# Three token groups share the first six slices of w_in; x of the third group at first in the place of the last four slices

## The chip, the cores and the metric

The kernel runs on one core of a Trainium2 chip. The metric is the device time of one execution in microseconds (us). Five runs of the kernel before took 668.6 to 671.58 us, median 669.63.

## The reference

A retention layer is followed by a feed-forward layer with SiLU. All inputs are float32 or wider; q, k and v have 4 batches, 8 heads, 768 positions and 64 features.

```python
for t in range(S):
    state = gamma * state + einsum('bhd,bhe->bhde', k[:, :, t], v[:, :, t])
    y[:, :, t] = scale * einsum('bhd,bhde->bhe', q[:, :, t], state)
x = y.transpose(0, 2, 1, 3).reshape(3072, 512)
h = x @ w_in                       # 512 x 2048
out = (h / (1 + exp(-h))) @ w_out  # 2048 x 512
```

## The kernel before, in words

The 768 positions are cut into six chunks of 128. One **unit** (c, b) is chunk c of batch b; there are 24 units, and the four units of a chunk make one **group** of 512 tokens. A **visit** (`visit`, L380) works on three units at once, in a pipeline: it transposes k and q of unit m (`stage_t`, TensorE, evacuated as kt and qt by ScalarE at L288), computes y of unit m-2 (`stage_y`), finishes that unit (`finish_y`), computes the scores sc of unit m-1 (`stage_a`, L334) and loads k and q two units ahead. So the units of group c are finished in visits 4c+2 to 4c+5.

[...] `split_x` (L359) makes from y the parts xh (ScalarE, L362), xl (VectorE, L363) and xm (VectorE, L364). All parts of one group's x lie in a tile xt of 128 x 3 x 4 x 512 words; the pool `xpool` has two of them. `take_w` converts a slice of the weights: `convert_w` (L172 to L186, one ScalarE and six VectorE instructions) turns 64-bit words into float32, and for w_in `split_w` (L105 to L110, two ScalarE and two VectorE instructions) splits it into wi. Slices 0 to 15 are the 16 slices of w_in, 16 to 31 those of w_out, which are only converted and written to memory (wod). Each w_in slice has its own place, tag `w0` to `w15`, in `wpool`; in the last group the split w_out slices (wo) take these places over, each after its last product.

`product_in(c, f)`, below product (c,f), multiplies group c with slice f: twelve matmuls of 512 columns into the PSUM tiles ha and hb (two of each), the first of which needs xh of all four units, the second xl and the third xm. ScalarE and VectorE evacuate them (L415, L416) into g, ScalarE applies Silu (L417), and `put_g` writes g to memory (gd, L423). The tile of g is one of three with the tag `hs` in `hpool`. After the last group, a second stage reads the g back, splits them (gs, L456 to L459) and multiplies with wo; it is not touched.

There are places for only two x tiles, and group 2 is finished in visits 10 to 13, before groups 0 and 1 are through. So group 2 is `LATE`: `finish_y` copies its y (ys, L348, a tile of tag `hs`) and writes it to memory (yd, L349); `late_x` (L371) later reads it back (yr, L375, again a tile of tag `hs`) and splits it into an xt tile, which is free once group 0 is through.

The order on TensorE is written by hand: it is the order of the calls. On ScalarE, VectorE, GpSimd and SyncE (SP, which issues the loads and most writes) a planner places the instructions when the kernel is built, the earlier traced first where several are ready; it may move them ahead of the calls around them. `issue_after(evac[0])` keeps a ScalarE instruction behind the last copy of qt that was traced. Each engine then works through its order strictly.

The order before: visits 0 to 5 with slices 0 to 3 come first. Then (0,0..7) with slices 4 to 10 and visits 6 to 10; (1,0..7) with slices 11 to 15 and visits 11 to 13; (0,8..15) with slices 16 and 17; (1,8..15) with slice 18, and `late_x` of unit 0 to 3 after (1,9), (1,10), (1,11) and (1,12). Groups 2 to 5 run through all 16 slices one after the other, with four visits in each and six slices of w_out in each of groups 2, 3 and 4, as far as there are any.

Of the kernel before, what the change touches and what calls it, by code (L numbers as in the profile page):

```python
# [13 lines left out]
FP32R = mybir.dt.float32r  # L14
U32 = mybir.dt.uint32
AF = mybir.ActivationFunctionType
# [10 lines left out]
HALF = 1.0 - 2.0 ** -13  # L27
# [4 lines left out]
def kernel(  # L32
# [26 lines left out]
    nc = tc.nc  # L59
    B, H, S, D = q.shape  # L60
    DM, DF = moe_w_in.shape
    C = 128
    NC = S // C
    HP = H // 2
    KIN = DM // 128
    NF = DF // 128
    NT = B * C
# [4 lines left out]
    scale = 1.0 / math.sqrt(D)  # L72
# [8 lines left out]
    wpool = pool("wpool", 1)  # L81
    xpool = pool("xpool", 2)
# [14 lines left out]
    def bits(x):  # L97
        return float(np.array(x, np.uint32).view(np.float32))

    def split_w(f, w32, name, factor):  # L100

        w = wpool.tile([128, 3, 512], FP32R, tag=f"w{f}", name=f"{name}{f}")
        lo = conv.tile([128, 512], FP32, tag="wl", name=f"{name}l_{f}")
        with tc.issue_after(evac[0]):
            nc.scalar.activation(out=w[:, 0, :], in_=w32, func=AF.Copy, scale=HALF * factor)  # L105
        high = w[:, 0, :].bitcast(FP32)
        nc.vector.scalar_tensor_tensor(out=lo, in0=w32, scalar=factor, in1=high,
                                       op0=ALU.mult, op1=ALU.subtract)
        nc.scalar.activation(out=w[:, 1, :], in_=lo, func=AF.Copy, scale=1.0 / EPS)
        nc.vector.scalar_tensor_tensor(out=w[:, 2, :], in0=high, scalar=EPS, in1=lo,  # L110
                                       op0=ALU.mult, op1=ALU.subtract)
        return w
# [73 lines left out]
        nc.vector.tensor_tensor(out=w, in0=s.bitcast(FP32), in1=p.bitcast(FP32), op=ALU.add)  # L186
        return w

    evac, w_sb = [], {}
    taken = [0]  # L190

    def take_w(between=lambda: None):
        i = taken[0]
        taken[0] += 1
        if i >= 2 * NF:
            return
        w32 = convert_w(i)
        between()
        if i < NF:
            w_sb[i] = split_w(i, w32, "wi", scale)  # L200
        else:
            nc.sync.dma_start(out=wo_dram[i - NF], in_=w32)
# [137 lines left out]
    def finish_y(n):  # L340
        c, b = units[n]
        sp, yp = live.pop(n)
        qt.pop(n)
        if b == 0 and c != LATE:
            xt[c] = xpool.tile([128, 3, KIN, NT], FP32R, tag="xt", name=f"xt_{c}")
        if c == LATE:
            y = hpool.tile([128, KIN, C], FP32, tag="hs", name=f"ys_{b}")
            nc.scalar.copy(out=y.rearrange("p (i o) t -> p i o t", o=2), in_=yp)  # L348
            nc.sync.dma_start(out=y_dram[b], in_=y)  # L349
            rest = None  # L350
        else:
            rest = split_x(c, b, yp)
        if c == 0:
            nc.scalar.copy(out=state[b], in_=sp)
        elif c < NC - 1:
            nc.vector.tensor_tensor(out=state[b], in0=state[b], in1=sp, op=ALU.add)
        return rest

    def split_x(c, b, y):  # L359
        xh, xl, xm = (xt[c][:, i, :, ts(b, C)].rearrange("p (i o) t -> p i o t", o=2)  # L360
                      for i in range(3))
        nc.scalar.activation(out=xh, in_=y, func=AF.Copy, scale=HALF)  # L362
        nc.vector.tensor_tensor(out=xl, in0=y, in1=xh.bitcast(FP32), op=ALU.subtract)  # L363
        return lambda: nc.vector.scalar_tensor_tensor(  # L364
            out=xm, in0=xl.bitcast(FP32), scalar=-1.0 / EPS, in1=xh.bitcast(FP32),
            op0=ALU.mult, op1=ALU.add)


    LATE = 2

    def late_x(b):  # L371
        if b == 0:
            xt[LATE] = xpool.tile([128, 3, KIN, NT], FP32R, tag="xt", name=f"xt_{LATE}")
        y = hpool.tile([128, KIN, C], FP32, tag="hs", name=f"yr_{b}")
        nc.sync.dma_start(out=y, in_=y_dram[b])  # L375
        split_x(LATE, b, y.rearrange("p (i o) t -> p i o t", o=2))()
# [3 lines left out]
    def visit():  # L380
        m = visits[0]
        visits[0] += 1
        if m - 2 >= len(units):
            return
        if m < len(units):
            stage_t(m)
        rest = None
        if m >= 2:
            stage_y(m - 2)
            rest = finish_y(m - 2)  # L390
        if 1 <= m <= len(units):
            stage_a(m - 1)
            scale_q(m - 1)
            scale_k(m - 1)
        if rest is not None:
            rest()
        load("k", m + 2)
        load("q", m + 2)
        load("v", m)
# [4 lines left out]
    def product_in(c, f):  # L404
        ha = ps_h.tile([128, 512], FP32, tag="ha", name=f"ha_{c}_{f}")
        hb = ps_h.tile([128, 512], FP32, tag="hb", name=f"hb_{c}_{f}")
        for kk in range(KIN):
            w = [w_sb[f][:, i, ts(kk, 128)] for i in range(3)]
            x = [xt[c][:, i, kk, :] for i in range(3)]
            first_, last = kk == 0, kk == KIN - 1  # L410
            nc.tensor.matmul(ha, lhsT=w[0], rhs=x[0], start=first_, stop=False)  # L411
            nc.tensor.matmul(ha, lhsT=w[1], rhs=x[1], start=False, stop=last)  # L412
            nc.tensor.matmul(hb, lhsT=w[2], rhs=x[2], start=first_, stop=last)  # L413
        hs = hpool.tile([128, NT], FP32, tag="hs", name=f"g_{c}_{f}")
        nc.scalar.activation(out=hs, in_=ha, func=AF.Copy, scale=ONE_E)  # L415
        nc.vector.tensor_tensor(out=hs, in0=hs, in1=hb, op=ALU.subtract)  # L416
        nc.scalar.activation(out=hs, in_=hs, func=AF.Silu)  # L417
        pending.append((c, f, hs))

    def put_g(keep):  # L420
        while len(pending) > keep:
            c, f, g = pending.pop(0)
            nc.sync.dma_start(out=g_dram[c, f], in_=g)  # L423
# [5 lines left out]
    def get(n):  # L429
        if n >= len(order):  # L430
            return
        c, f = order[n]
        name = "kqk"[n % 3]
        g = ld.tile([128, NT], FP32, tag=f"{name}f", name=f"gr_{c}_{f}",
                    bufs=4 if name == "k" else 2)
        nc.sync.dma_start(out=g, in_=g_dram[c, f])
        got[n] = g

    def get_w(f):
        if f < NF:  # L440
            t = stage.tile([128, DM], FP32, tag="wf", name=f"wr_{f}")
            nc.sync.dma_start(out=t, in_=wo_dram[f])
            w_got[f] = t
# [3 lines left out]
    def split(n):  # L447
        if n >= len(order):
            return
        c, f = order[n]  # L450
        get(n + G_AHEAD)
        g = got.pop(n)
        if f % 4 == 0:
            blocks[n // 4] = xpool.tile([128, 3, 4, NT], FP32R, tag="xt", name=f"gs_{c}_{f}")
        t = blocks[n // 4][:, :, f % 4, :]
        nc.scalar.activation(out=t[:, 0, :], in_=g, func=AF.Copy, scale=HALF)  # L456
        high = t[:, 0, :].bitcast(FP32)
        nc.vector.tensor_tensor(out=t[:, 1, :], in0=g, in1=high, op=ALU.subtract)  # L458
        nc.vector.scalar_tensor_tensor(out=t[:, 2, :], in0=t[:, 1, :].bitcast(FP32),  # L459
                                       scalar=-1.0 / EPS, in1=high,  # L460
                                       op0=ALU.mult, op1=ALU.add)
        ready[n] = t
# [8 lines left out]
    for m in range(1, B + 2):  # L471
# [2 lines left out]
            take_w()  # L474
        if m == 2:
            first_chunk()
    half = NF // 2
    phases = ((0, 0, (0, 1, 2, 3, 5), (0, 1, 2, 3, 4, 5, 6)),
              (1, 0, (1, 3, 5), (0, 1, 2, 3, 5)),
              (0, half, (), (2, 6)),  # L480
              (1, half, (), (7,)))
    for c, f0, at, takes in phases:
        for i in range(half):
            product_in(c, f0 + i)
            if i in takes:
                take_w()
            put_g(1)
            if i in at:
                visit()
            if (c, f0) == (1, half) and 1 <= i <= B:  # L490
                late_x(i - 1)
    for c in range(2, NC):
        for f in range(NF):
            product_in(c, f)
            if c < NC - 1 and f % 3 == 0:
                take_w()
            put_g(1)
            if f % 4 == 1:
                visit()
            if c == NC - 1:  # L500
                if f == 0:
                    get_w(0)
                    get_w(1)
                wo[f] = split_w(f, w_got.pop(f), "wo", 1.0)
                get_w(f + 2)
                if f >= NF - 6:
                    if f == NF - 6:
                        for n in range(G_AHEAD):
                            get(n)
                    if f >= NF - S_AHEAD:  # L510
                        split(f - NF + S_AHEAD)
    put_g(0)

    for c in range(NC):
# [56 lines left out]
```

## Time and profile before

| | |
|---|---|
| median of five runs | 669.63 us |
| the profiled execution | 669.77 us, span of its core 667.9 us |
| TensorE (PE) busy | 634.4 us, 95% |
| VectorE (DVE) busy | 424.3 us, 64% |
| ScalarE (ACT) busy | 281.8 us, 42% |
| mean granted TensorE clock | 0.992 |
| first product (0,0) starts | 40.26 us |

The profile shows one execution. Times are us from the start of the span. An instruction's line names the line of the kernel, the tile that it writes and the one that it reads (without their numbers: xt is any x tile, wi any w_in slice), and behind it, in brackets, how long its engine sat idle before it and what ended that. "PE" is TensorE's matmuls; their printed lengths overlap, so the distance of two starts is what one costs. The page cuts the span into 40 slices of 16.7 us, each digit the busy tenths of an engine. A busy average over the span says little here, as the stages differ.

### The profile page before, as it was taken

To read this page: it belongs to the slowest core of one execution; us is meant where nothing else is said; L and a number is where in the kernel's file an instruction comes from. 1 tells how busy PE (TensorE), PEld (TensorE's weight loads), DVE (VectorE), ACT (ScalarE), POOL (GpSimd) and SP (SyncE) were. 2 spreads that over 40 slices of the span, in tenths; PEclk is the share of its full clock that TensorE was granted. 3 is DMA by queue.
4 is the path that set the end of the run, shared out by engine and by line. 5 is a ranking of instruction groups with operands and counts; after the bars stand their busy time and mean duration, and the time that the engine had idled before them with its cause. 6 is when DMAs were issued, how large, how long until landed. Compare 5 with 4: busy or idle time off the path is not lost.

```text
span 667.9 us, 11107 instructions
## 1 busy us (share of the span) xinstructions
PE 634.4 (95%) x4288; PEld 518.6 (78%) x4288; DVE 424.3 (64%) x696; ACT 281.8 (42%) x510; POOL 10.5 (2%) x44
## 2 busy tenths in 40 slices
PE   4769988999999999999999999999999999999996
PEld 3657767787788888888888888888888888888885
DVE  4898999995558686866347777363555454544631
ACT  5535566554545444444436883132131312221311
POOL 3000000000000000000000000000000000000000
PEclk9979989999999999999999999999999999999999
DMA  9976767865456676755324664252333342523401
GB/s 205 196 163 168 186 189 195 236 227 211 142 174 204 181 222 185 219 176 189 126 80 143 221 196 140 74 162 91 126 126 127 110 143 75 177 82 107 159 0 64
DMA packets 123061, 103.50 MB, mean 155 GB/s; under 512 B 80000, under 2 KB 88192, under 8 KB 123008
## 3 DMA queue, kind: packets, MB, share of 16 engines
q1 hardware_dynamic: 119552, 96.49, 49.2%
q10 hardware_dynamic: 3456, 6.29, 2.5%
q8 instruction: 34, 0.56, 0.3%
q14 instruction: 19, 0.16, 0.1%
HBM read 66.06 MB, written 36.70 MB: 154 GB/s over the span
## 4 chain that ended last, share of the span: by engine, by line
PE 69%; DVE 12%; DMA 8%; ACT 6%; issue 3%; SPq 1%; ACTq 0%; DVEq 0%
PE ha L411 8%; PE hb L413 8%; PE ha L412 8%; PE ob L533 7%; PE o L533 6%; PE o L532 6%; PE o L531 6%; PE oa L531 6%; PE oa L532 6%; DMA wf<-in_moe_w_in_dram 3%; PE y L303 2%; DVE g L416 2%; PE tp L285 2%; DMA gd<-g 1%; DVE am L338 1%
## 5 line engine op out<-in xcount | busy, mean ns | idle before, releaser
L413 PE MATMUL hb<-xt,wi 128*128 128x512 f32 x384 | 151.4, 394 | 4.2 <-DVE xt L364 3.5
L411 PE MATMUL ha<-xt,wi 128*128 128x512 f32 x384 | 153.0, 398 | 0.4 <-ACT g L415 0.4
L412 PE MATMUL ha<-xt,wi 128*128 128x512 f32 x384 | 150.7, 392 | 0.0
L458 DVE TENSOR_TENSOR gs<-gr,gs 128x512 fp32r<-128x512 f32 x96 | 62.1, 686 | 93.4 <-ACT gs L456 93.4
L456 ACT ACTIVATE gs<-gr 128x512 fp32r<-128x512 f32 x96 | 53.3, 620 | 139.2 <-issue 131.9
L416 DVE TENSOR_TENSOR g<-g,hb 128x512 f32<-128x512 f32 x96 | 65.7, 684 | 60.5 <-ACT g L415 59.9
L413 PEld LDWEIGHTS hb<-xt,wi 128*128 128x128 f32 x384 | 72.5, 189 | 22.5 <-DVE xt L364 3.8
L417 ACT ACTIVATE g<-g 128x512 f32<-128x512 f32 x96 | 60.6, 632 | 69.5 <-DVE g L416 69.4
L411 PEld LDWEIGHTS ha<-xt,wi 128*128 128x128 f32 x384 | 72.5, 189 | 19.1 <-issue 3.6
L412 PEld LDWEIGHTS ha<-xt,wi 128*128 128x128 f32 x384 | 72.5, 189 | 14.7 <-DVE xt L363 0.3
L415 ACT ACTIVATE g<-ha 128x512 f32<-128x512 f32 x96 | 56.8, 591 | 54.2 <-PE ha L412 36.2
L533 PE MATMUL ob<-wo,gs 128*128 128x512 f32 x192 | 75.3, 392 | 0.0
L533 PE MATMUL o<-wo,gs 128*128 128x512 f32 x192 | 74.8, 390 | 0.0
L531 PE MATMUL oa<-wo,gs 128*128 128x512 f32 x192 | 74.8, 390 | 0.0
L532 PE MATMUL oa<-wo,gs 128*128 128x512 f32 x192 | 74.8, 390 | 0.0
L531 PE MATMUL o<-wo,gs 128*128 128x512 f32 x192 | 74.8, 390 | 0.0
L532 PE MATMUL o<-wo,gs 128*128 128x512 f32 x192 | 74.8, 390 | 0.0
L459 DVE SCALAR_TENSOR_TENSOR gs<-gs 128x512 fp32r<-128x512 f32 x96 | 61.9, 685 | 0.0
L533 PEld LDWEIGHTS ob<-wo,gs 128*128 128x128 f32 x192 | 36.1, 188 | 9.0 <-DVE o L539 1.7
L531 PEld LDWEIGHTS oa<-wo,gs 128*128 128x128 f32 x192 | 36.1, 188 | 7.6 <-ACT o L538 0.2
L532 PEld LDWEIGHTS o<-wo,gs 128*128 128x128 f32 x192 | 36.1, 188 | 7.5
L533 PEld LDWEIGHTS o<-wo,gs 128*128 128x128 f32 x192 | 36.1, 188 | 7.5
(67 smaller groups left out, 684.8 us busy)
## 6 DMA issues: line engine op xcount, KB each, us to landing
gd<-g SPq DMA_DIRECT2D x96, 256.0 KB, 3.0
gr<-gd SPq DMA_DIRECT2D x96, 256.0 KB, 2.7
wf<-in_moe_w_out_dram SPq DMA_DIRECT2D x16, 512.0 KB, 3.6
kf<-in_k_dram SPq DMA_DIRECT2D x24, 256.0 KB, 4.3
qf<-in_q_dram SPq DMA_DIRECT2D x24, 256.0 KB, 4.1
vf<-in_v_dram SPq DMA_DIRECT2D x24, 256.0 KB, 4.4
out_dram<-o ACTq DMA_DIRECT2D x24, 256.0 KB, 2.1
wf<-in_moe_w_in_dram SPq DMA_DIRECT2D x16, 256.0 KB, 3.1
```

Source lines behind the costliest of these rows:

```text
L411: nc.tensor.matmul(ha, lhsT=w[0], rhs=x[0], start=first_, stop=False)
L412: nc.tensor.matmul(ha, lhsT=w[1], rhs=x[1], start=False, stop=last)
L413: nc.tensor.matmul(hb, lhsT=w[2], rhs=x[2], start=first_, stop=last)
L415: nc.scalar.activation(out=hs, in_=ha, func=AF.Copy, scale=ONE_E)
L416: nc.vector.tensor_tensor(out=hs, in0=hs, in1=hb, op=ALU.subtract)
L417: nc.scalar.activation(out=hs, in_=hs, func=AF.Silu)
L456: nc.scalar.activation(out=t[:, 0, :], in_=g, func=AF.Copy, scale=HALF)
L458: nc.vector.tensor_tensor(out=t[:, 1, :], in0=g, in1=high, op=ALU.subtract)
L459: nc.vector.scalar_tensor_tensor(out=t[:, 2, :], in0=t[:, 1, :].bitcast(FP32), scalar=-1.0 / EPS, in1=high, op0=ALU.mult, op1=ALU.add)
L531: nc.tensor.matmul(oa, lhsT=gh, rhs=wo[f][:, 0, :], start=first_, stop=False)
L532: nc.tensor.matmul(oa, lhsT=glo, rhs=wo[f][:, 1, :], start=False, stop=last)
L533: nc.tensor.matmul(ob, lhsT=gm, rhs=wo[f][:, 2, :], start=first_, stop=last)
```

## The change

The 16 slices of w_in get 12 places of their own and one shared place `wq` of four slices, for slices 12 to 15; it has the size of one x tile. Group 2's x is split at once, as that of the other groups, into this place, and group 2 runs its first six products from there. After these, slices 12 to 15 are split into the place. y of group 2 is still written to memory, and read back and split a second time into an x tile, for its other ten products. The copy ys in on-chip memory is what the first split reads.

The order is now: (0,0..5), (1,0..5), (2,0..5), (0,6..10), (1,6..10), (0,11..15), (1,11..15), (2,6..15), then groups 3 to 5 as before. Visits 6 to 9 stand in the first of these, 10 to 13 in the second, 14 to 17 in the last. The slices are taken later: 4, 5, 6 in (0,0..5), 7 and 8 in (1,0..5), 9 and 10 in (2,0..5), then two in each of the next three stretches; slices 17 to 20 of w_out go beside (2,6..15), and the last five beside group 4. `late_x` follows (1,12), (1,13), (1,14) and (1,15). For slices 12 to 15 the first ScalarE instruction of the split is held behind the last traced xh in place of the last copy of qt; in the last group, the four w_out slices in `wq` can be written only when (5,15) is through with all four.

```diff
+    quads = {}
+    def w_slot(f, name):
+        if f < NF - 4:
+            return wpool.tile([128, 3, 512], FP32R, tag=f"w{f}", name=f"{name}{f}")
+        if f == NF - 4:
+            quads[name] = wpool.tile([128, 4, 3, 512], FP32R, tag="wq", name=f"{name}4")
+        return quads[name][:, f - NF + 4]
...
-        w = wpool.tile([128, 3, 512], FP32R, tag=f"w{f}", name=f"{name}{f}")
+        w = w_slot(f, name)
-        with tc.issue_after(evac[0]):
+        with tc.issue_after(held[0] if f >= NF - 4 else evac[0]):
...
-        if b == 0 and c != LATE:
-            xt[c] = xpool.tile([128, 3, KIN, NT], FP32R, tag="xt", name=f"xt_{c}")
+        if b == 0:
+            p, tag = (wpool, "wq") if c == LATE else (xpool, "xt")
+            xt[c] = p.tile([128, 3, KIN, NT], FP32R, tag=tag, name=f"xt_{c}")
         if c == LATE:
             y = hpool.tile([128, KIN, C], FP32, tag="hs", name=f"ys_{b}")
-            nc.scalar.copy(out=y.rearrange("p (i o) t -> p i o t", o=2), in_=yp)
+            y4 = y.rearrange("p (i o) t -> p i o t", o=2)
+            nc.scalar.copy(out=y4, in_=yp)
             nc.sync.dma_start(out=y_dram[b], in_=y)
-            rest = None
-        else:
-            rest = split_x(c, b, yp)
+            yp = y4
+        rest = split_x(c, b, yp)
...
-        nc.scalar.activation(out=xh, in_=y, func=AF.Copy, scale=HALF)
+        held[:] = [nc.scalar.activation(out=xh, in_=y, func=AF.Copy, scale=HALF).ins]
...
-    phases = ((0, 0, (0, 1, 2, 3, 5), (0, 1, 2, 3, 4, 5, 6)),
-              (1, 0, (1, 3, 5), (0, 1, 2, 3, 5)),
-              (0, half, (), (2, 6)),
-              (1, half, (), (7,)))
+    for c, f, takes, at in ((0, range(6), (0, 2, 5), (0, 1, 3, 4)),
+                            (1, range(6), (2, 5), (0, 1, 3, 4)),
+                            (2, range(6), (1, 4), ()),
+                            (0, range(6, 11), (7, 9), ()),
+                            (1, range(6, 11), (7, 9), ()),
+                            (0, range(11, NF), (11, 13), ()),
+                            (1, range(11, NF), (), ()),
+                            (2, range(6, NF), (6, 9, 12, 15), (6, 8, 11, 13))):
...
-            if (c, f0) == (1, half) and 1 <= i <= B:
-                late_x(i - 1)
+        if c == 1 and NF - B <= f:
+            late_x(f - NF + B)
```

More of the change, by code (lines that the diff above doesn't have):

```diff
@@ L187, in convert_w @@
         return w
-    evac, w_sb = [], {}
+    evac, held, w_sb = [], [], {}
     taken = [0]
@@ L476 @@
             first_chunk()
-    half = NF // 2
-    phases = ((0, 0, (0, 1, 2, 3, 5), (0, 1, 2, 3, 4, 5, 6)),
-              (1, 0, (1, 3, 5), (0, 1, 2, 3, 5)),
-              (0, half, (), (2, 6)),
-              (1, half, (), (7,)))
[L482 to L489, printed above, removed]
-            if (c, f0) == (1, half) and 1 <= i <= B:
-                late_x(i - 1)
@@ L492 @@
-    for c in range(2, NC):
-        for f in range(NF):
[L494 to L511, printed above, removed]
+    steps = {}
@@ new lines @@
+    for c, f, takes, at in ((0, range(6), (0, 2, 5), (0, 1, 3, 4)),
[6 more added lines that the diff above has]
+                            (2, range(6, NF), (6, 9, 12, 15), (6, 8, 11, 13))):
+        for i in f:
+            steps[c, i] = i in takes, i in at
@@ new lines @@
+    for c in range(3, NC):
+        for f in range(NF):
+            steps[c, f] = c < NC - 1 and f % 3 == 0, f % 4 == 1
+    for (c, f), (takes, at) in steps.items():
+        product_in(c, f)
+        if takes:
+            take_w()
+        put_g(1)
+        if at:
+            visit()
+        if c == 1 and NF - B <= f:
+            late_x(f - NF + B)
+        if c == NC - 1:
+            if f == 0:
+                get_w(0)
+                get_w(1)
+            wo[f] = split_w(f, w_got.pop(f), "wo", 1.0)
+            get_w(f + 2)
+            if f >= NF - 6:
+                if f == NF - 6:
+                    for n in range(G_AHEAD):
+                        get(n)
+                if f >= NF - S_AHEAD:
+                    split(f - NF + S_AHEAD)
```

## The prediction

> **What bounds the kernel now.** I read the page first, then the busy time by stretch, then TensorE's order of time with its waits, then those of SP and VectorE. The page gives TensorE 95%, and its slices say where the rest is:
>
> ```profile
> PE 634.4 (95%) x4288; PEld 518.6 (78%) x4288; DVE 424.3 (64%) x696; ACT 281.8 (42%) x510; POOL 10.5 (2%) x44
> ...
> PE   4769988999999999999999999999999999999996
> ...
> DVE  4898999995558686866347777363555454544631
> ...
> PEclk9979989999999999999999999999999999999999
> ```
>
> The chain that ended last is 69% TensorE, 12% VectorE (DVE). The average hides the stage of the change: TensorE is short of 9 in the slices up to 133 us, and there DVE shows 8 and 9. The table by stretch (busy us and instruction count for PE, PEld, DVE, ACT, POOL, then the clock and DMA) says it in us:
>
> ```profile
> 40.00:60.00 20.00, 15.38 (x180) 11.94 (x172) 16.90 (x28) 9.95 (x18) 0.00 (x0) 0.91 0.68 156
> 60.00:80.00 20.00, 18.92 (x250) 15.67 (x251) 19.59 (x36) 11.01 (x20) 1.36 (x1) 1.00 0.77 194
> 80.00:100.00 20.00, 17.73 (x142) 14.53 (x141) 19.06 (x34) 11.62 (x21) 0.00 (x0) 0.91 0.68 192
> ...
> 120.00:140.00 20.00, 18.68 (x152) 15.08 (x151) 19.37 (x35) 12.58 (x23) 1.09 (x1) 1.00 0.73 220
> ...
> 160.00:180.00 20.00, 19.50 (x84) 15.04 (x83) 9.55 (x15) 10.44 (x18) 0.00 (x0) 1.00 0.42 141
> 180.00:300.00 120.00, 119.39 (x1082) 98.24 (x1081) 84.64 (x142) 55.71 (x98) 2.19 (x2) 1.00 0.65 194
> ```
>
> From 60 to 140 DVE is full (18.6 to 19.6 of 20); from 180 on TensorE idles 0.6 us in 120. So only 40 to 140 can be won. Its waits (last bracket: idle, releaser), four of them:
>
> ```profile
> 44.75 0.50 PE L413 MATMUL hb<-xt,wi 128*128 128x512 f32 x1 [3.53 <-DVE xt L364]
> ...
> 52.96 1.10 PE L334 MATMUL sc<-qt,kt 64*64 64x128 f32 x32 [1.06 <-ACT qt L288]
> ...
> 86.93 1.96 PE L334 MATMUL sc<-qt,kt 64*64 64x128 f32 x32 [2.27 <-ACT qt L288]
> ...
> 115.51 1.10 PE L334 MATMUL sc<-qt,kt 64*64 64x128 f32 x32 [1.79 <-ACT qt L288]
> ```
>
> The first lies before anything that the change moves. The sc matmuls of visits 6 to 13 wait 1.06, 0, 0.98, 0, 2.27, 0.26, 1.79 and 1.31 us, 7.7 in all: ScalarE's copy of qt stands in its queue behind a Silu or a w split that waits for the full DVE. After the 2.27 the matmuls run at half rate until 90.27 (starts 0.43 apart, not 0.23), about 1.5 us more.
>
> **The early part: DVE load.** From rows: product 12 x 0.227 = 2.73 us of TensorE and 0.68 of DVE; visit 4.15 (64.00 to 69.13 less its wait), 4.28 with the slower first matmul behind it. A w_in slice costs DVE eight ops (0.44+0.42+0.69+0.42+0.70+0.68+0.69+0.69) = 4.7 us; a visit am 1.22, qt, kf, xl, xm 0.69 each, state 0.41 = 4.4; for group 2 it was 3.0 without the x split. Before, (0,0..7) asks DVE for 8 x 0.68 + 7 x 4.7 + 4 x 4.4 + 3.0 = 59 us beside 8 x 2.73 + 5 x 4.28 = 43 of TensorE. After: w4 is done at 49.7 as now, so (0,0..5) has w5, w6 and four visits, 4.1 + 9.4 + 17.6 = 31 beside 33.5; (1,0..5), the four added splits in it (4 x 1.37 DVE, 4 x 0.59 ACT), 31 beside 33.5; (2,0..5) 13.5 beside 16.4; (0,6..10) 12.8 beside 13.7. DVE fits, at 92%.
>
> - **Visit waits.** Bounds: only the 1.06 of visit 6 stays (ScalarE loads a table there), -6.6, or all stay, 0. I take 3.0 left (1.06 and seven of 0.28, the size of the 0.26 row), since visits still come in pairs: **-4.7**.
> - **The slow stretch at 87** goes with its gap: **-1.5** (0 if another gap replaces it).
> - **New joints.** (1,0) and (2,0) follow one product after the visit that ends their x. TensorE needs xm 4.15 + 2.86 + 0.46 = 7.5 us after the visit starts; xm ended 6.0 after (visit 14, quiet DVE), 7.0 (visit 6) and 11.6 (visit 9, full DVE). For (2,0) add 0.6, as x is split from the copied y. Bounds 0 and 4.1 + 4.7; slices w6 and w8 are fenced behind the visit's qt copy, so near visit 6: **+0.5**.
> - **Slices in time.** w8 to w15 may run back to back after visit 13 (w_out slice 19, traced after (2,0) at 179, finished at 156, so slices move ahead). At 6.4 us each (w13, w14, w15 ended 6.3 and 6.5 apart) and 5 for the visit, w15 is there 56 us after visit 13 starts; (0,15) starts at 4.28 (the visit) + 2.73 for (1,5) + 16.4 for (2,0..5) + 27.3 for (0,6..10) and (1,6..10) + 10.9 for (0,11..14) = 61.7. **0**; at 7.4 each (as 89.72 to 97.13) 2.5.
> - **Shared place.** w12's first ScalarE op waits for the last matmul of (2,5), and behind it stand evacuations; two buffers of ha and hb cover it: **0**, at most one product, 2.7. In the last group the four w_out splits wait for (5,15) and are needed 12 x 2.73 = 33 us later: **0**; their 9.6 us of DVE and ACT work there cost at most the 7 us that ScalarE now idles at 404. Five w_out slices move into group 4, as dense then as groups 2 and 3: 0.1. No DMA is added; input loads come as densely as now, with fewer w_in loads between them.
>
> **The late part: x of group 2, second time.** This decides. Every read yr takes one of three buffers that it shares with the g of each product, in program order: the buffer of the tile three before. SP's order shows it (gd is a g's write, yr a read back):
>
> ```profile
> 162.75 0.32 SPq L375 DMA_DIRECT2D yr<-yd  x1
> 163.33 0.32 SPq L423 DMA_DIRECT2D gd<-g  x1
> 166.92 0.32 SPq L375 DMA_DIRECT2D yr<-yd  x1
> 168.18 2.88 SPq L423 DMA_DIRECT2D gd<-g  x2
> 171.16 1.91 SPq L375 DMA_DIRECT2D yr<-yd  x2
> ```
>
> Each yr starts 4.1, 3.6, 3.0 and 2.0 us after the write of the g three before (158.70, 163.33, 168.18, 170.74), though y lay ready since 131. The reads are not moved ahead. The last split then ends here:
>
> ```profile
> 176.53 0.68 DVE L363 TENSOR_TENSOR xt<-yr,xt 128x512 fp32r<-128x512 f32 x1
> 177.24 0.69 DVE L364 SCALAR_TENSOR_TENSOR xt<-xt 128x512 fp32r<-128x512 f32 x1
> ```
>
> (0,15) ended at 155.8, so x of group 2 takes 22.1 us from there. Now eight products (1,8..15) cover it, and (2,0) starts at 179.08: 1.1 us to spare. After the change the reads follow (1,12) to (1,15), again the second to fifth product after (0,15), so the pattern is the same; but only five products stand before (2,6). Five products took 14.1 us here (starts 155.8 and 169.9), and hb comes 0.46 later: 22.1 - 14.6 = **+7.5**. Bounds: from the end of (1,14), shortest rows (L415 0.55, L416 0.6, Silu 0.6, write 2.0, read 2.6, three split ops 1.9, hand-overs 0.5) give 8.8, so 4 x 2.73 + 0.5 + 8.8 - 14.6 = +5.6; with the first read's 4.1 in place of 2.0, +9.6. Nobody is hidden behind it: every engine waits for TensorE then.
>
> After such a gap the clock falls: the matmuls from 46.0 to 49.7 ran at half rate after 3.53 us idle, and PEclk shows 0.91 in that stretch: **+1.7** (1.5 to 1.9 by the two rows; 0 if the first two matmuls of (2,6) break the gap). The small late waits between 166 and 176 (1.3 us) are in part later than (1,13), where group 2 now waits anyway: **-0.8**.
>
> [...]
>
> **The sum**: -4.7 - 1.5 + 0.5 + 7.5 + 1.7 - 0.8 = +2.7. The profiled execution took 669.77 (span 667.9 and 1.87 around it), near the median of 669.63; so 672.5 on its scale, **672.3** on the median's.
>
> **Rivals.**
> - *x in time* (faster): the reads are issued early enough for xm to end within 14.6 us of (0,15), the point from which it decides. Then 669.8 - 4.7 - 1.5 + 0.5 - 0.8 = 663.3. For it: slices do move 22 us ahead. Against: with free buffers between 104 and 110 no yr moved. Chance 0.12.
> - *All early waits gone, chain at its shortest*: 669.8 - 6.6 - 1.5 + 5.6 + 0.9 - 0.8 = 667.4. For it: visits after 180 wait almost nothing. Against: 92% DVE. 0.17.
> - *The early part stays full*: order on DVE is still tight at the joints: visits -1.5, joints +3.0, rest as forecast: 669.8 - 1.5 - 1.5 + 3.0 + 7.5 + 1.7 - 0.8 = 678.2. This holds too if the slices are pulled ahead and the change spreads nothing. 0.23.
> - *Forecast*, 671 to 675.5: 0.48.
>
> Changes under 0.3% (2.0 us) can't be told from none. Faster: 0.12 + 0.09 of the second = 0.21; same: 0.08 + 0.12 of the forecast's lower end = 0.20; slower 0.59. The range 666 to 678.5 leaves out the first rival and the last one's upper part, some 0.2.
>
> **What would show it.** TensorE's wait list should show one gap of 5 to 9 us at the first product of (2,6), released by xt at L362 to L364, with four yr before it; sc waits on qt of about 3 us up to 160; no DVE stretch over 19 of 20. The forecast is wrong if that gap is under 3 us, or if xt waits of more than 3 us stand at (1,0) and (2,0).

## The result and the profile after

The changed kernel takes 671.45 us (median of 27 runs, 670.01 to 673.18) beside 669.95 us of the kernel before (50 runs). The ratio is 1.0021, 95% interval 1.0015 to 1.0027: slower by about 1.4 us. The interval excludes 1, but the effect is hardly larger than the 1.15 us by which the median of the kernel before alone differs between this set of runs and the later ones. The forecast was 672.3 in a range of 666 to 678.5. Two large effects of opposite sign stand behind the small number.

The page of the changed kernel, in the same rows as before:

```profile
PE 632.4 (95%) x4288; PEld 518.6 (78%) x4288; DVE 430.1 (64%) x704; ACT 284.2 (43%) x514; POOL 10.1 (2%) x44
...
PE   3769999999979999999999999999999999999996
...
DVE  4897888999446786868667749373555454544631
...
PEclk9979999999979999999999999999999999999999
```

TensorE's slices from 50 to 117 us, which were 8 and 9, are all 9 now. One slice far from there, 183 to 200 us, has fallen to 7, and the clock with it. VectorE does eight instructions more, the two of each added split. By stretch (busy us and count for PE, PEld, DVE, ACT, POOL, then clock and DMA):

```profile
60.00:80.00 20.00, 19.04 (x241) 15.64 (x234) 16.58 (x29) 8.52 (x16) 1.04 (x1) 1.00 0.71 177
80.00:100.00 20.00, 19.13 (x225) 15.83 (x224) 16.84 (x27) 10.12 (x18) 0.00 (x0) 1.00 0.66 177
...
140.00:160.00 20.00, 20.00 (x90) 16.58 (x89) 19.45 (x36) 13.77 (x25) 0.00 (x0) 1.00 0.56 183
...
180.00:200.00 20.00, 15.25 (x80) 11.66 (x80) 9.39 (x14) 8.12 (x14) 0.00 (x0) 0.83 0.34 109
```

From 60 to 100 VectorE is busy 16.6 to 16.8 of 20 us, where it was 19.1 to 19.6. Its full stretch has moved to 140 to 160, where TensorE runs products only and is never idle. So the load was moved to where nothing waits for it. What TensorE still waits for is short to list (last bracket: idle time and releaser; line numbers are higher by 10 to 12 than before):

```profile
44.67 0.79 PE L425 MATMUL hb<-xt,wi 128*128 128x512 f32 x1 [3.03 <-DVE xt L375]
52.60 1.10 PE L344 MATMUL sc<-qt,kt 64*64 64x128 f32 x32 [1.09 <-ACT qt L298]
70.08 1.10 PE L344 MATMUL sc<-qt,kt 64*64 64x128 f32 x32 [0.96 <-ACT qt L298]
87.56 1.10 PE L344 MATMUL sc<-qt,kt 64*64 64x128 f32 x32 [0.87 <-ACT qt L298]
117.09 0.50 PE L425 MATMUL hb<-xt,wi 128*128 128x512 f32 x1 [1.45 <-DVE xt L375]
192.41 0.79 PE L423 MATMUL ha<-xt,wi 128*128 128x512 f32 x1 [4.75 <-ACT xt L373]
```

The list runs from the first product to (2,6); waits of less than 0.2 us are left out in it and in the sums. The sc waits of visits 6 to 13 are 2.92 us, against 7.67. The last two lines are new: a wait at (2,0) for xm of unit 11, and one of 4.75 us at (2,6) for the second split of group 2. SP's queue shows how the latter comes about (yr is a read of y, gd a write of g):

```profile
179.08 0.37 SPq L387 DMA_DIRECT2D yr<-yd  x1
181.38 0.32 SPq L435 DMA_DIRECT2D gd<-g  x1
183.07 0.32 SPq L387 DMA_DIRECT2D yr<-yd  x1
184.33 2.82 SPq L435 DMA_DIRECT2D gd<-g  x2
187.25 1.96 SPq L387 DMA_DIRECT2D yr<-yd  x2
```

The pattern of before has come back, later by about the distance of the calls: a read, a write, a read, two writes, two reads. The fourth read is issued at 188.89, 2.1 us after the write of g(1,14) at 186.83. But (1,15) ends at 187.5, and VectorE finishes the split only here:

```profile
192.39 0.69 DVE L374 TENSOR_TENSOR xt<-yr,xt 128x512 fp32r<-128x512 f32 x1 [0.39 <-ACT xt L373]
193.11 0.69 DVE L375 SCALAR_TENSOR_TENSOR xt<-xt 128x512 fp32r<-128x512 f32 x1
```

xm is there at 193.80, and hb starts at 193.86, 5.9 us later than without a wait. Then the matmuls start 0.43 us apart, not 0.23, until 197.8: 1.9 us more. The page counts 4.75 of these 7.8 us as idle; the rest hides in "busy" matmuls, because the first three, 0.72 apart, wait for xh, xl and xm in turn.

### The profile page after: what moved, and what is told of

It is laid out like the page before. It is cut to its first block, busy times and chain, and to the rows that moved or that the text cites. A ratio compares the mean times of both kernels' runs of the same rounds, so it can differ in the third digit from the quotient of the medians.

```text
span 667.8 us, 11108 instructions
## 1 busy us (share of the span) xinstructions
PE 632.4 (95%) x4288; PEld 518.6 (78%) x4288; DVE 430.1 (64%) x704; ACT 284.2 (43%) x514; POOL 10.1 (2%) x44
## 4 chain that ended last, share of the span: by engine, by line
PE 79%; DVE 4%; ACT 3%; DMA 1%; issue 1%; ACTq 0%; SPq 0%; DVEq 0%
PE ha L423 12%; PE hb L425 11%; PE ha L424 11%; PE ob L547 7%; PE o L547 6%; PE o L546 6%; PE o L545 6%; PE oa L545 6%; PE oa L546 6%; PE y L313 3%; PE sc L344 2%; PE tp L295 1%; DMA yr<-yd 1%; DVE g L428 1%; ACT g L429 1%
```

## The experiments

The theory to be tested: the reads of y are late because they take turns with the g in three buffers, in program order, and the early gain comes from VectorE being asked for less there. All kernels below ran beside the kernel before, whose median there was 671.1 us, 1.15 above the 669.95 from which the expectations were reckoned; each expected time is read with that shift. Ratios are to the kernel before.

To read the profiles alike, the starts of TensorE's matmuls are summed up: a product costs 2.73 us and a visit 4.15 us without any wait, and what goes beyond is its excess, idle time and slow matmuls together.

### One product earlier

```diff
-        if c == 1 and NF - B <= f:
-            late_x(f - NF + B)
+        if c == 1 and NF - B - 1 <= f < NF - 1:
+            late_x(f - NF + B + 1)
```

> The changed kernel with the read-back and second split of group 2's x one product earlier, after (1,11) to (1,14). Buffer theory (each read waits for the buffer of the g three allocations before it, so the last xm comes some 9 us after the product two before it): everything at (2,6) moves 2.7 us earlier; the wait until xm falls from 5.9 to 3.2 us, the half-rate stretch behind it stays near 1.9; time 671.45 - 2.7 = 668.7, a little faster than before. Rival (the ten operations of the second split, or the place of x that group 0 frees, take the time, wherever the reads stand): the wait stays near 5.9 us and the time at 671.5.

Measured 669.8 us, ratio 0.9979 (0.9970 to 0.9989), expected 668.7 + 1.15 = 669.9. The excess of (1,15) and (2,6) together fell from 7.8 to 5.4: the wait until xm from 5.9 to 4.0, where 3.2 was expected, and the slow stretch behind it from 1.9 to 1.4 (matmuls 0.43 apart again):

```profile
191.82 0.51 PE L423 MATMUL ha<-xt,wi 128*128 128x512 f32 x1 [2.79 <-ACT xt L373]
```

The wait moves with the calls. That already speaks against the split's own work or the place of x, which would have kept the wait near 5.9.

### Buffers apart

```diff
-        y = hpool.tile([128, KIN, C], FP32, tag="hs", name=f"yr_{b}")
+        y = conv.tile([128, KIN, C], FP32, tag=("ca", "cs", "cp", "wl")[b], name=f"yr_{b}")
```

> The changed kernel with the four read-back tiles in the four conversion tiles (free between the conversions of two w_out slices) in place of the three that the products' g go through; the calls stand where they stood. Buffer theory: the reads are issued before (0,15) ends, the four splits need some 5 to 8 us from there, and (2,6) starts without a wait or half-rate stretch: 5.9 + 1.9 = 7.8 us less, 663.6. One or two w_out slices are converted later, which nothing waits for. Rival (the split work itself or the freed place decides): the wait stays above 4 us and the time above 669.

Measured 663.65 us, ratio 0.9885 (0.9867 to 0.9904); expected 664.8 with the shift. The trace lists no wait of TensorE between 119 and 226 us. Not a call was moved; only the buffers differ, and the reads are issued while group 0 still runs:

```profile
166.31 0.32 SPq L387 DMA_DIRECT2D yr<-yd  x1
...
170.33 1.03 SPq L387 DMA_DIRECT2D yr<-yd  x2
...
172.93 0.32 SPq L387 DMA_DIRECT2D yr<-yd  x1
```

The four splits then end at 183.4, 7.7 us after (0,15) and 5.9 us before (2,6). So neither their work nor the place that group 0 frees was short. The w_out slices that share the conversion tiles come later and nothing waits for them. This run shows the cause, and it beats both kernels.

### The kernel before, with late reads alone

```diff
-            if (c, f0) == (1, half) and 1 <= i <= B:
-                late_x(i - 1)
+            if (c, f0) == (1, half) and half - B <= i:
+                late_x(i - half + B)
```

> The kernel before, with one thing of the change alone: the read-back follows (1,12) to (1,15), the last four products before group 2, in place of (1,9) to (1,12). Buffer theory: a wait of 5 to 7.5 us at (2,0), released by xt, and 1.5 to 1.9 us of half rate; the small late waits go (up to -2.2): 669.95 + 4.5 to 8, so 674.5 to 678, likeliest 676. Rival (the wait at (2,6) comes from the shared place or from the order of the slices, which are absent here): no wait above 2 us at (2,0), 669 to 671.

Measured 678.44 us, ratio 1.0101 (1.0083 to 1.0120); expected 677.2 with the shift. The same gap stands at (2,0), with nothing else of the change in the kernel:

```profile
184.05 0.79 PE L411 MATMUL ha<-xt,wi 128*128 128x512 f32 x1 [5.27 <-ACT xt L362]
```

With its slow stretch it is 8.4 us. The shared place and the new order of the slices are not needed to make it.

### The slices taken early again

```diff
-    for c, f, takes, at in ((0, range(6), (0, 2, 5), (0, 1, 3, 4)),
-                            (1, range(6), (2, 5), (0, 1, 3, 4)),
-                            (2, range(6), (1, 4), ()),
+    for c, f, takes, at in ((0, range(6), (0, 1, 2, 3, 4, 5), (0, 1, 3, 4)),
+                            (1, range(6), (0, 1), (0, 1, 3, 4)),
+                            (2, range(6), (), ()),
```

> The changed kernel with slices 4 to 9 taken in (0,0..5) and 10, 11 after (1,0) and (1,1), that is two or three slices per pair of visits as before the change; later slices as in the change, w_out one or two slices earlier. Load theory (the visits waited because VectorE had more work than TensorE): VectorE is asked for 50 us beside 33.5 in the first stretch, is full again, and the sc waits come back: +4 to +8 us, 675.5 to 679.5. Rival (the new spacing of the visits alone removed the waits, or the slices are not pulled forward by the order on the queues): within 1.5 us of 671.45.

Measured 682.1 us, ratio 1.0161 (1.0142 to 1.0180), 10.4 us above the changed kernel beside the same median of before (671.68, below): more than either theory said. VectorE is full again from 60 to 80, but the dearest wait is not an sc wait:

```profile
60.00:80.00 20.00, 18.31 (x248) 14.81 (x242) 19.55 (x34) 12.11 (x22) 0.91 (x1) 1.00 0.77 183
```
```profile
88.92 0.79 PE L425 MATMUL hb<-xt,wi 128*128 128x512 f32 x1 [3.71 <-DVE xt L375]
```

That is the joint at (1,0), one product behind the visit that ends its x: 6.7 us with the slow matmuls. Visits 8, 11 and 12 wait 1.6, 0.8 and 1.7 for qt; visit 10 runs 0.6 over with no wait listed, at the end of the slow stretch. So the load theory holds, and the expectation missed that a full VectorE hits the new joint harder than the visits.

### xm ahead of the scores

A visit called xm last, behind the score product and the scaling of qt and kf. Here it comes right after xl:

```diff
             rest = finish_y(m - 2)
+            rest()
...
-        if rest is not None:
-            rest()
```

> The changed kernel with the last part of a visit's x split (xm) called right after xl, ahead of the score product, the scaling of qt and kf. Order theory (the wait of 1.45 us at (2,0), and part of the 3.0 to 3.5 us wait at the first product, come from xm standing behind am, qt and a slice operation in VectorE's queue, not from too little time for it): the wait at (2,0) goes, 1.7 us with its tail, and the first one shrinks by 1.2 to 1.8; time -3.2, about 668.3; am comes 0.6 us later and is needed only at the next visit. Rival (VectorE is simply late there, whatever the order): both waits stay within 0.5 us, time within 1 us of 671.45.

Measured 667.93 us, ratio 0.9954 (0.9940 to 0.9967); expected 669.5 with the shift. The wait at (2,0) is gone, and the first wait of all, which the change never touched, is a third of what it was:

```profile
42.67 0.50 PE L424 MATMUL hb<-xt,wi 128*128 128x512 f32 x1 [1.18 <-DVE xt L375]
```

The half-rate stretch behind it is gone too, the matmuls start 0.23 us apart: the excess of the first product is 1.8, where the changed kernel's two profiles have 4.8 and 6.2. The queue of VectorE in the changed kernel shows the order: xm of unit 11 reads what xl wrote by 114.1, and starts 2.2 us later:

```profile
113.42 0.68 DVE L374 TENSOR_TENSOR xt<-ys,xt 128x512 fp32r<-128x512 f32 x1
114.02 0.68 DVE L193 SCALAR_TENSOR_TENSOR cp<-wf,cp 128x512 f32<-128x512 uint32 x1
114.62 1.22 DVE L348 TENSOR_TENSOR am<-sc,decay 128x1024 f32<-128x1024 f32 x1
115.75 0.68 DVE L288 TENSOR_TENSOR qt<-qt,gq 128x512 f32<-128x512 f32 x1
116.35 0.69 DVE L375 SCALAR_TENSOR_TENSOR xt<-xt 128x512 fp32r<-128x512 f32 x1
```

So the wait at (2,0) and most of the first one were a matter of order in VectorE's queue. The repair has a price: six products between 114 and 152 us run 0.2 to 0.4 us longer each, 1.9 in all (2.0 with both repairs, below), which the expectation did not have. The gain of 3.7 us in the medians, against 3.2 expected, is therefore not the sum of the two waits alone; how the rest is made up is not shown.

### The changed kernel again, and both repairs together

> The changed kernel itself once more, beside the next two on the same chip. Buffer theory: a wait of 4.7 to 5.5 us at (2,6), then a half-rate stretch, together 7.5 to 8.7 us over a normal product; time 1.0021 of before. The profiled execution before this one was near the low end of its runs; what differs between executions should be the cost of the half-rate stretches after the two long gaps (at the start and at (2,6)), not any wait of the queues.

Measured 671.68 us, ratio 1.0015 (1.0004 to 1.0027). Its profiled execution (670.34 us) has the same waits on qt, and at (2,6) 8.1 us where the first one had 7.8.

> The changed kernel with both: read-back tiles in the conversion tiles, and xm called ahead of the scores. If the waits are as separate as the theories say, the two gains add: 663.65 - 3.2 = 660.5. If the removed wait at (2,0) only moves to the next shortage (the sc waits of the visits, or w slices that are not split in time), 662 to 664.

Measured 659.4 us, ratio 0.9830 (0.9815 to 0.9845); expected 661.7 with the shift. The two gains, 8.0 and 3.7 us over the changed kernel, add up to 11.8; measured 12.3. This is the fastest kernel of the study.

### The kernel before with both repairs

> The kernel before with the two repairs of the last runs and nothing of the change: read-back tiles in the conversion tiles, xm called right after xl. It asks whether the change itself is still worth something once both have the repairs. Load theory: the first wait shrinks as in the changed kernel (about -3.3 with its half-rate tail), the small late waits go (up to -2.2), but the sc waits of visits 8 to 13 behind a full VectorE (8 us with their half-rate stretch) stay: 669.95 - 3.3 - 1.5 = 665, about 5.5 us above the changed kernel with both repairs. Rival (the early gain of the change was mostly a matter of order, which the repair of xm gives as well): 659 to 661, no better or worse than the changed kernel with both.

The edits are those of the two repairs. Measured 664.75 us, ratio 0.9909 (0.9891 to 0.9927); expected 666.2 with the shift. It is 5.4 us above the changed kernel with both repairs, where 5.5 were expected. Its visits still stand behind a full VectorE (19.5 to 19.9 of each 20 us from 60 to 120, where the changed kernel with both repairs has 16.6 to 17.8), here visit 13; in visits 8 and 9 it is now y that waits, 1.4 and 0.9 us for am, which the repair has put behind xm:

```profile
122.23 1.98 PE L334 MATMUL sc<-qt,kt 64*64 64x128 f32 x32 [2.67 <-ACT qt L288]
```

So the change, apart from its late reads, is worth some 5 us even beside the repairs, and the late reads hid it.

## Why the prediction was right

The sign, the mechanism and the size held. That the total is so close is in part luck: the terms miss by up to 1.6 us, and the joints and the slow stretch miss the other way than the rest. Set against the two first profiled executions (669.77 before, 669.84 after), term by term:

| term | forecast | measured |
|---|---|---|
| visits 7 to 13, sc waits and the slow stretch at 87 | -4.7 - 1.5 = -6.2 | excess 8.2 to 1.2 = -7.0 |
| joints (1,0) and (2,0) | +0.5 | 0 and +1.7 |
| wait at (2,6) until xm | +7.5 | +5.9 |
| half rate behind it | +1.7 | +1.9 |
| small waits of products between 133 and 179 | -0.8 | 2.2 to 0 = -2.2 |
| the first product and visit 6 | 0 | -1.0, but starts 0.65 later: -0.4 |
| sum | +2.7 | about 0; by the ratio of the medians +1.4 |

- **Visits.** The 3.0 us left in sc waits were 2.92. That of visit 6 stayed, 1.09 us for 1.06; an ACT_TABLE_LOAD of 1.28 us on ScalarE stands ahead of its copy of qt in both profiles. The load table was right: w slices moved off the visits' stretch, and the run with early slices brought the load and the waits back. One sign did not come true: VectorE has a stretch over 19 of 20, 19.45 at 140 to 160, where it does no harm.
- **Joints.** This term was too small by a factor of three. The forecast took (1,0) and (2,0) as alike but for the copy of y. At (1,0) nothing waited. At (2,0) xm stood behind am, qt and a slice operation in VectorE's queue; calling xm first removed the wait with the copy in place. What the copy alone adds was not measured.
- **The wait at (2,6).** The step was right: same pattern of reads, three products fewer to hide it. The listed idle time of 4.75 us is just under the 5 that were named as the sign; until xm it is 5.9. The term was oversized by 1.6 us. The forecast carried over the 22.1 us from the end of (0,15) to xm; after the change it was 19.9. The chain begins sooner: before, VectorE was converting a w_out slice when (0,15) ended, and g(0,15) was written 2.9 us, the first read issued 7.0 us after that; after the change it is 2.0 and 5.2, and the last read keeps that lead (17.0 against 15.0). The cover became shorter too, as the five products took 13.6 us in place of 14.1. From the end of (1,14) it took 9.0 us, close to the 8.8 that the forecast had as its lower end.
- **Half rate.** 1.9 after 4.75 us idle. The run with earlier reads paid 1.4 after 2.8 us.
- **Small late waits.** They went altogether, not in part. The forecast counted only those from 166 to 176, at (1,12), (1,14) and (1,15), 1.4 us by the starts, where the reads' splits stand between the evacuations; after the change the first two splits run beside (1,13) to (1,15) without holding them up, and no product runs beside the last two. The 0.8 us at (0,8) and (0,15) stood behind work on slices in VectorE's queue, and the forecast left them out.
- **Slices and the shared place.** Costed at nothing, and nothing waited for either: no wait for wi, and none for wo when the second stage starts.
- **Readings.** Two in the working are wrong and change no term: the page shows TensorE short of 9 up to 117 us, not 133; and the upper bound of +9.6 at (2,6) adds the 2.1 us to the 7.5, not to the shortest rows, which would give +7.7.

The first profiled execution of the changed kernel is as fast as that of the kernel before, while the ratio of the medians gives 1.4 us. In the profiles the excess of the first product and visit 6 ranges from 5.8 to 7.4 us among kernels with the same order up to there, and that of the gap at (2,6) from 7.8 us (that execution) to 8.6 (early slices). That execution has the lowest of both. The granted clock of each run points the same way: of the changed kernel's runs, the five with a mean of 0.990 or 0.991 have a median of 670.2 us, the sixteen with 0.985 or 0.986 one of 671.7. That the half-rate stretches make up the whole difference is likely but not shown.

## What to carry to other kernels

When work is moved, ask of each transfer in it which buffer it takes and whose turn comes before: a read whose data had been written over 60 us before was late because its buffer went round with the results of the very products that were to hide it. A stage that is full on one engine and a stage that has room can be balanced by moving work between them, but then the cover that the moved order took from another chain has to be counted again, in products. Where a gain is expected and the total hardly moves, sum the excess over the undisturbed step, stage by stage; the repair of the one bad stage was worth 8 us here.

## What the runs showed that was not expected

Three waits of TensorE between 2.27 and 2.79 us were followed by matmuls at half rate, but the length of a wait alone does not decide it. Waits of 1.18 (with xm ahead), 1.58 (changed kernel, at 23 us) and 1.79 us (before, at 115) were followed by the full rate, with starts 0.23 us apart or sc matmuls of 1.10 us, while the three of 2.27 (before, at 87 us), 2.67 (at 122, the kernel before with both repairs) and 2.79 us (reads one product earlier) were followed by starts 0.43 us apart, or by sc matmuls of 1.96 and 1.98 us.

Ahead of the first product stands a wait of 2.33 us in the kernel before (32.47 to 34.80) and one of 2.34 us in the first profile of the changed kernel. Behind them the granted clock is 0.50, from 35.80 to 39.21 and from 37.27 to 40.68, and y matmuls take 1.92 us in place of 1.05. In the second profile of the changed kernel the clock stays at 1.00 there, and the scores before the first product take 1.10 us, where the first profile has 1.82. Here are two stretches of 3.41 us each, as long as the half clock lasted, first of the kernel before, then of the second profile of the changed kernel; the first busy time is TensorE's, the third number from the end the clock:

```profile
32.39:35.80 3.41, 1.08 (x12) 0.86 (x8) 3.38 (x6) 1.38 (x3) 0.00 (x0) 1.00 0.82 205
35.80:39.21 3.41, 2.84 (x33) 2.43 (x32) 3.34 (x6) 1.07 (x2) 0.00 (x0) 0.50 0.79 139
```
```profile
30.75:34.16 3.41, 1.91 (x49) 1.50 (x44) 3.02 (x6) 2.25 (x4) 0.00 (x0) 1.00 0.50 135
34.16:37.57 3.41, 2.01 (x32) 1.78 (x34) 3.41 (x6) 1.45 (x3) 0.00 (x0) 1.00 1.18 229
```

In the first the stretch with the wait has TensorE busy for 1.08 us, and the next has half the clock. In the second the two stretches are busy for 1.91 and 2.01 us, and both have the full clock. That it is a matter of where a wait of 2 to 3 us falls is the author's reading of these profiles; no run tested it. The first product's waits of 1.18, 1.19 and 1.20 us, in the three profiles with xm ahead, were each followed by starts 0.23 us apart.
